# Spectral mix with a gated convolution: small transfers in place of the last row's products, a new order of work

## The chip, the core and the metric

The kernel runs on one core of one Trainium2 chip. The core has five engines with a queue of instructions each, which they work through in order: TensorE (PE in the profile; its weight loads are PEld), VectorE (DVE), ScalarE (ACT), GpSimd (POOL) and SyncE (SP, which here only issues DMA transfers). The metric is the device time of one execution in microseconds (us), as the median of several runs. One execution was also taken by the profiler; all rows shown come from that one.

## The reference

Two results are computed from the same input x (2048 positions, 512 channels, f32) and mixed by a gate:

```python
    x = A_x
    g = _sigmoid((x * gate_w).sum(-1, keepdims=True))
    a = _A_ref(x, A_w_r, A_w_i)     # rfft2, times a complex weight, irfft2
    b = _B_ref(x, ...)              # causal convolution over positions, plus x * D_skip
    return g * a + (1 - g) * b
```

The kernel of the convolution in b is made of 128 decaying exponentials for each channel. The program computes on the chip how many channels have exponents small enough (a bound on the exponent over all 2048 positions, below 2^-25) for the convolution to be a running sum of x times one number for each channel. With these inputs all channels do, and the general branch behind `tc.If(n_small < D)` isn't entered.

## The kernel before

Everything is f32. The two-dimensional transform a is done by matrix products. The work is cut into steps, each a small Python function that emits its instructions, and the order is written out by hand in the string `PLAN`: a letter for the step, then its numbers (which unit, then which buffers). `D6.1.0` is step D of unit 6, with PSUM bank 1 and block buffer 0. The order of the words is the order in each engine's queue; there is no other schedule. Waits between engines follow from the data. PSUM is used as four banks of two 512-column halves each, `ps0` to `ps3`. The block buffers (`pairs`, 8 KB a partition; `blk(i)` is half of one) and the `shorts` are shared by many steps, so a step also waits until the former user of its buffer is done.

The stages, in terms of the letters:

- `A` loads x in ten parts into GI; `C` (TensorE, line 233) makes the first transform along the positions, eight products of 128x128 for each of eight units, and `c` (ScalarE, line 238; one as `f` on VectorE) copies the bank to E1. All eight copies must be there before any `D`.
- `D` (line 248) transforms along the channels, eight products for each of eight units; `E` (253) copies the bank; `P` (269) finishes the transform along the positions into a bank; a ninth, half-sized unit (8) takes part from P on. `d` (275) copies two of a bank's eight parts; `Z` (290, 291, VectorE) forms sums and differences in place in the bank.
- `W` and `U` (311, 316, 317, VectorE) multiply by the complex weight, which `l` (299) has loaded into the part of GI that x no longer needs. Partition 127 of that weight, the row of channel frequencies 0 and 256, comes from a small extra table `hT` (steps `J`), which `L` (303, 305) puts in place with a small transfer from SP.
- `p` (321) adds the two halves of the weighted product by an accumulating DMA that GpSimd issues. `g` (328, 329, GpSimd) makes two sums and differences from it, 128x512 each.
- `I` (338, 339, 341, TensorE) transforms back along the channels. For partition 127 the sums of g aren't right: frequency 0 and frequency 256 share that row and need the bare parts and not their sums. So the matrix `dbw` has zeros in that row for the even outputs, and two further products (341) with 32 rows and 64 columns, from the uncombined data and the matrix `dbl`, bring the row in. `i` (346, ScalarE) copies the bank to GI.
- `B`, split for three units into `Y` and `b` (357, 358, 363), `T` (367, VectorE transposes), and `Q` (476) transform back along the positions; `q` (481, 482) adds the convolution's part and stores the result. Q multiplies by matrices that carry the gate: `a` loads their base, `K` (397, VectorE) multiplies by the gate, `k` (403, ScalarE) makes four copies with signs.
- The convolution: `X` loads x again with channels on partitions (XT), `m` (436, VectorE) makes the running sum, `s` (439, ScalarE) scales it, and two forms add it to XT times the skip term: `e` and `o` (442, VectorE, for two of the four channel groups), or `v` and `w` (445, ScalarE, scaling XT) and `M` (449, an accumulating DMA issued by GpSimd, for the other two groups). `H` (453, GpSimd) multiplies by 1 - g, eight times 128x1024. Every `q` needs all eight H.
- The gate: `G0` (375, TensorE) sums x times gate_w, `G1` (378, 379, ScalarE) takes g and 1 - g, `G2` stores both to DRAM (g by four transfers of scattered elements) and loads 1 - g broadcast to all partitions (`hg`); `G3` (389) loads g broadcast.
- `R`, `r` load constants and parameters; `N` decides which channels are small.

Of the kernel before, what the change touches and what calls it, by code (L numbers as in the profile page):

```python
# [15 lines left out]
P = 128  # L16
# [3 lines left out]
NPAIR = 8  # L20
# [20 lines left out]
def _consts():  # L41
# [100 lines left out]
def body(ctx: ExitStack, tc: tile.TileContext, x, xg, xt, w, wh, prms, vecs, gw, dskip,  # L142
# [19 lines left out]
    gd = wst.enter_context(tc.tile_pool(name="gdram", bufs=1, space=bass.MemoryType.DRAM)).tile([2, L], F32, name="gd")  # L162
# [33 lines left out]
    with tc.manual_schedule():  # L196
# [12 lines left out]
        def load_p(k, i):  # L209
# [9 lines left out]
            lambda: (nc.sync.dma_start(dbw, c_dbw[:, :, 0:2]), nc.sync.dma_start(dbl, c_dbw[96:P, :, 2])),  # L219
# [81 lines left out]
        def load_h(u, n):  # L301
            if u == 8:
                nc.sync.dma_start(wtile(8)[P - 1:P, :, :, 0].rearrange("p r a k -> p (r a) k"), hT[8:9, :, :64])
            else:
                nc.sync.dma_start(GI[P - 1:P, 8 * u:8 * u + 8 * n].rearrange("p (u n o) t -> p u n o t", n=4, o=2)[:, :, :, 0], hT[u:u + n])
# [16 lines left out]

        def g_a(u, i):
# [6 lines left out]

        def I_(u, i):
            m = nrow(u) // 64
            p = t_["pi", u] = bank(i).rearrange("p v (n t) -> p v n t", t=P)
            gt = t_["gt", u].rearrange("p h m c k -> p h m (c k)")
            px = t_["t", u][96:P, 0].rearrange("p x a (m k) -> p x a m k", k=64)
            for v in range(m):
                for h in range(2):
                    T.matmul(p[:, v, 2 * h + 1], gt[:, h, m + v], dbw[:, h, 1], start=True, stop=True)  # L338
                    T.matmul(p[:, v, 2 * h], gt[:, h, v], dbw[:, h, 0], start=True, stop=False)  # L339
                    for c in range(2):  # L340
                        T.matmul(p[64 * c:64 * c + 64, v, 2 * h], px[:, c ^ h, h, v], dbl[:, h], start=False, stop=True, tile_position=(96, 64 * c))  # L341
# [35 lines left out]
        def G1():  # L377
            S.activation(gsg[:, 0].rearrange("p (b a) -> p b a", a=16), t_["pg"].rearrange("p (a b) -> p b a", a=16), AF.Sigmoid)
            S.activation(gsg[:, 1], t_["pg"], AF.Sigmoid, scale=-1.0)

        def G2():
            nc.sync.dma_start(gd[1].rearrange("(j n) -> j n", j=4), gsg[0:P:32, 1])
            nc.sync.dma_start(hg, gd[1].rearrange("(o n) -> o n", o=1).broadcast_to([P, L]))
            for j in range(4):
                nc.sync.dma_start(gd[0].rearrange("(k b h a) -> k h b a", k=2, h=2, a=16)[j // 2, j % 2:j % 2 + 1], gsg[32 * j:32 * j + 1, 0].rearrange("p (b a) -> p b a", a=16))
# [49 lines left out]
        def scan(q):  # L435
            V.tensor_tensor_scan(run[:, q % 2, 1:1025], XT[:, 0, q], XT[:, 1, q], 0.0, op0=ALU.add, op1=ALU.add)  # L436
# [311 lines left out]
```

## Time and profile before

| | us |
|---|---|
| Median of 3 runs (lowest, highest) | 134.47 (134.28, 134.53) |
| The profiled execution | 134.16 |
| Its span in the profile | 132.4 |
| VectorE busy | 82.2 |
| ScalarE busy | 51.2 |
| GpSimd busy | 56.2 |
| First product starts | 4.86 |
| Last H ends, first q starts | 113.64, 113.67 |

The span runs from the first instruction to the last; the device time has 1.76 us more around it. A row of a timeline reads: start, duration, engine, line, operation, what it writes and reads, how many of them, and in brackets how long the engine was idle before and on what it waited. A `q` behind the engine's name (SPq) is the queue's own work, such as issuing a DMA; SP's time for issuing one is the duration shown, and the transfer lands later. A row of a window reads: start and end, its length, then each engine's busy time in it (PE, PEld, DVE, ACT, POOL in this order), the granted TensorE clock, the share in which the DMA engines were busy, and GB/s. A row of groups reads: line, engine, operation, tiles, shape, count, then busy time and the mean duration of one in ns, then idle time before them.

### The profile page before, as it was taken

The page shows a single profiled execution, that of the slowest core. Times are in us where ns is not written, and L with a number is a line of the kernel's source. Part 1 is how long each engine was busy: PE and PEld are TensorE (multiplying, and loading weights), DVE is VectorE, ACT ScalarE, POOL GpSimd, SP SyncE. Part 2 cuts the span into 40 slices and gives each one's busy share as a digit, 9 for nine tenths or more (in the row PEclk, how much of TensorE's full clock was granted, in tenths as well). Part 3 has the DMA queues.
Part 4 walks back from the last instruction along what each step waited for, and adds up shares of the span by engine and source line. Part 5 has one row for each costly group of instructions (what it writes and reads, how often), then busy time and mean ns, then how long its engine had stood idle before and what let it go on. Part 6 is the DMA issues. An engine that isn't in the chain of part 4 may idle for free.

```text
span 132.4 us, 2360 instructions
## 1 busy us (share of the span) xinstructions
PE 117.2 (89%) x944; PEld 95.5 (72%) x944; DVE 82.2 (62%) x101; ACT 51.2 (39%) x63; POOL 56.2 (42%) x49
## 2 busy tenths in 40 slices
PE   0599998999979999989999999999999999999700
PEld 0599997999879998858736766777655339999600
DVE  0031036078299999788770099999999573677610
ACT  3033635444267542313164113349679970000000
POOL 0000000001040840586798919499949999300000
PEclk9999999999999999999999999999999999999965
DMA  2999989996869789998667769990969600099660
GB/s 83 349 396 384 392 309 272 389 389 136 314 195 223 253 238 276 274 386 174 126 130 147 141 144 316 295 335 10 191 131 198 124 5 7 9 368 396 267 245 5
DMA packets 10643, 29.85 MB, mean 226 GB/s; under 512 B 1818, under 2 KB 2938, under 8 KB 10366
## 3 DMA queue, kind: packets, MB, share of 16 engines
q1 hardware_dynamic: 8606, 22.99, 48.4%
q0 software_dynamic: 1872, 6.55, 25.9%
q8 instruction: 9, 0.15, 0.4%
q10 hardware_dynamic: 144, 0.07, 0.4%
q14 instruction: 12, 0.10, 0.2%
HBM read 18.82 MB, written 4.21 MB: 174 GB/s over the span
## 4 chain that ended last, share of the span: by engine, by line
PE 69%; DMA 15%; DVE 7%; POOL 2%; issue 2%; ACT 1%
PE ps L233 13%; PE ps L476 12%; PE ps L357 11%; PE ps L338 9%; PE ps L341 8%; DMA blk<-blk 8%; PE ps L339 5%; PE ps L269 4%; DMA short<-in_prms_dram 3%; DMA GI<-in_x_dram 3%; PE ps L248 3%; PE ps L375 3%; DVE ps L290 2%; DVE ps L291 2%; DVE blk L316 1%
## 5 line engine op out<-in xcount | busy, mean ns | idle before, releaser
L233 PE MATMUL ps<-s,GI 128*128 128x128 f32 x128 | 17.4, 307 | 4.9 <-DMA GI<-in_x_dram 4.9
L453 POOL TENSOR_TENSOR XT<-XT,hg 128x1024 f32<-128x1024 f32 x8 | 20.9, 3038 | 0.0
L233 PEld LDWEIGHTS ps<-s,GI 128*128 128x128 f32 x128 | 17.2, 222 | 4.8 <-DMA s<-in_c_s_dram 4.8
L346 ACT COPY GI<-ps 128x1024 f32<-128x1024 f32 (+1 forms) x9 | 8.7, 964 | 24.2 <-PE ps L341 24.2
L328 POOL TENSOR_TENSOR blk<-blk 128x512 f32<-128x512 f32 (+1 forms) x9 | 13.0, 1443 | 11.6 <-DMA blk<-blk 11.2
L248 PE MATMUL ps<-dfw,E 128*128 128x128 f32 x128 | 15.6, 277 | 2.2 <-DVE blk L317 1.6
L248 PEld LDWEIGHTS ps<-dfw,E 128*128 128x128 f32 x128 | 14.8, 192 | 2.9 <-DVE blk L317 2.0
L338 PE MATMUL ps<-dbw,blk 128*128 128x128 f32 x68 | 16.3, 322 | 0.6 <-POOL blk L329 0.6
L269 PE MATMUL ps<-s2e,blk 128*128 128x128 f32 x136 | 16.8, 277 | 0.0
L269 PEld LDWEIGHTS ps<-s2e,blk 128*128 128x128 f32 x136 | 15.8, 192 | 1.2 <-issue 0.8
L357 PE MATMUL ps<-GI,s2p 128*64 128x512 f32 (+1 forms) x64 | 15.7, 583 | 0.0
L436 DVE TENSOR_TENSOR_SCAN run<-XT 128x1024 f32<-128x1024 f32 x4 | 11.2, 2803 | 6.7 <-DMA XT<-in_xt_dram 6.7
L476 PE MATMUL ps<-blk,E 128*128 128x128 f32 x128 | 15.3, 282 | 0.0
L476 PEld LDWEIGHTS ps<-blk,E 128*128 128x128 f32 x128 | 15.2, 196 | 0.1
L341 PE MATMUL ps<-last,blk 32*64 32x128 f32 x136 | 14.8, 293 | 0.0
L338 PEld LDWEIGHTS ps<-dbw,blk 128*128 128x128 f32 x68 | 10.1, 188 | 5.8 <-issue 5.0
L415 POOL TENSOR_TENSOR few<-few 128x4 f32<-128x4 f32 x1 | 0.2, 202 | 31.5 <-ACT few L412 31.5
L339 PE MATMUL ps<-dbw,blk 128*128 128x128 f32 x68 | 13.1, 275 | 0.0
L481 DVE TENSOR_TENSOR blk<-ps,XT 128x1024 f32<-128x1024 f32 x8 | 9.6, 1222 | 5.6 <-PE ps L476 2.8
L329 POOL TENSOR_TENSOR blk<-blk 128x512 f32<-128x512 f32 (+1 forms) x9 | 12.6, 1404 | 0.0
L238 ACT COPY E<-ps 128x1024 f32<-128x1024 f32 x7 | 7.1, 1012 | 13.7 <-PE ps L233 13.7
L311 DVE TENSOR_TENSOR blk<-ps,GI 128x1024 f32<-128x1024 f32 (+1 forms) x9 | 10.5, 1164 | 3.1 <-PE ps L341 1.8
(51 smaller groups left out, 142.7 us busy)
## 6 DMA issues: line engine op xcount, KB each, us to landing
XT<-in_xt_dram SPq DMA_DIRECT2D x4, 1024.0 KB, 6.6
GI<-in_w_dram SPq DMA_DIRECT2D x8, 512.0 KB, 3.9
blk<-blk POOLq DMA_DIRECT2D x8, 512.0 KB, 5.7
out_dram<-blk SPq DMA_DIRECT2D x8, 512.0 KB, 3.3
GI<-in_x_dram SPq DMA_DIRECT2D x6, 512.0 KB
XT<-run POOLq DMA_DIRECT2D x4, 512.0 KB, 5.9
GI<-in_x_dram SPq DMA_DIRECT2D x4, 256.0 KB, 5.4
hg<-gd SPq DMA_DIRECT2D x1, 1024.0 KB
```

Source lines behind the costliest of these rows:

```text
L233: T.matmul(p[:, u, :, j], X[:, 8 * k + 4 * u + j], s1, start=True, stop=True)
L248: T.matmul(p[:, n], E1[:, 8 * u + n], dfw[:, n % 4], start=True, stop=True)
L269: T.matmul(p[:, h, :, o, 64 * v:64 * v + 64], t_["e2", u % 8][:, 4 * v + 2 * h + o], st[:, ::-1] if h else st, start=True, stop=True)
L328: G.tensor_tensor(gt[:, :, :, 0], t[:, 0:4:3], t[:, 1:3], op=ALU.add)
L329: G.tensor_tensor(gt[:, ::-1, :, 1], t[:, 0:4:3], t[:, 1:3], op=ALU.subtract)
L338: T.matmul(p[:, v, 2 * h + 1], gt[:, h, m + v], dbw[:, h, 1], start=True, stop=True)
L339: T.matmul(p[:, v, 2 * h], gt[:, h, v], dbw[:, h, 0], start=True, stop=False)
L341: T.matmul(p[64 * c:64 * c + 64, v, 2 * h], px[:, c ^ h, h, v], dbl[:, h], start=False, stop=True, tile_position=(96, 64 * c))
L357: T.matmul(p[64 * s:64 * s + 64, u, :16 * n], s2p[:, 0, g], GI[:, 32 * s:32 * s + n, tt], start=True, stop=s == 1, tile_position=(0, 64 * s))
L436: V.tensor_tensor_scan(run[:, q % 2, 1:1025], XT[:, 0, q], XT[:, 1, q], 0.0, op0=ALU.add, op1=ALU.add)
L453: G.tensor_tensor(o, o, hg[:, 1024 * (k % 2):1024 * (k % 2) + 1024], op=ALU.mult)
L476: T.matmul(p[:, u, :, j], E4[:, b // 16, b % 16, :, u], t_["q", b // 8][:, 8 * u + b % 8].rearrange("p q a -> p (q a)"), start=True, stop= ...
```

## The change

Each word below says what the new program does in place of the old.

- **Zeros first.** `gsg` is cleared, and two products of 128x128 by 128x512 on it go to bank 3 before the plan starts.
- **Last row by small transfers.** `dbw` has its full rows again, `dbl` and line 341 are gone, so I is eight products for each full unit. A new step `h` runs between g and I: four transfers from SP, each of one partition, copy the uncombined parts over partition 127 of g's result.
- **L from ScalarE's queue** and not SP's.
- **Four sums on GpSimd.** For units 0, 1, 2 and 8 a new step `j` adds the halves by a GpSimd sum (128x1024, for unit 8 128x512) in place of the accumulating DMA `p`.
- **Skip terms by adding transfers.** The plan uses `v`, `w` and `M` for all four channel groups, and `e` and `o` for none. The running sums take block buffers (the tile `run` is gone, and there is a ninth pair of them). Since the shifted sum has no leading zero column any more, M of the even positions starts at the second column.
- **Gate turned on ScalarE.** Only 1 - g is computed, stored and broadcast. G3 makes g in the order that K wants with two copies `1 - hg` on ScalarE.
- **New order.** The plan is rewritten: all parts of x go out first, then XT 0, 3, 2, 1; C runs in the order 4, 3, 6, 1, 5, 7, 2, 0; D, P, W and I begin with 1, 2, 5, 3, 0; Q begins with 1, 3, 7.

```diff
-NPAIR = 8
+WARM = 2
+NPAIR = 9
...
-R0 A4 C3.0 A7 C6.1 r0.0 A3 c3 C2.0 r1.1 N0 A5 R3 J0 A6 C4.2 R8 A9 A8 c6 c2 C5.0 c4 f5 A1 C7.1 c7 A2 C1.0 R4 c1 A0 C0.1
...
-U3 G2 p3 g0.2 I4.3 a0.0 G5 Z8 W8.4 i4 I2.0 i2 a1.1 a2.2 I0.2 i0 U8 p8 g3.0 o0 e0 m2 e1 a3.3 g8.1 o1 I3.0 v2 s2 w2 i3
...
+R0 A5 C4.0 A4 A7 R4 A2 A6 C3.1 A9 A3 A0 A8 A1 c4 c3 X0 C6.0 R3 C1.1 X3 R1 R6 c1 X2 C5.2 c6 C7.1 m0.0 C2.0 c5 c7 X1 l2
+l1 c2 C0.1 c0 J0 r1.0 J1.0 m3.1 r0.1 D1.1.2 J2 E1 D2.0.3 E2 m2.4 R8 D5.1.5 m1.6 R10 r2.2 R2 P2.0 l0 l4 d2.3 l8 l3 l5
+l6 Z2 L1.2 N0 D3.2.7 E3 P1.3 G0.2 d1.3 N1 W2.8 U2 E5 N3 P3.0 G1 L3.2 D0.1.2 D4.2.3 d3.0 Z1 R5 W1.7 j2 E0 U1 R7 Z3 L0
+s1 g2.7 l7 P0.1 E4 j1 d0.0 W3.6 w1 v1 P5.3 U3 D6.0.8 G2 g1.9 Z0 W0.5 U0 h2 d5.0 Z5 L5.3 p3 D7.2.5 E6 M1 E7 P6.0 W5.8
+U5 h1 j0 w2 I1.1 d6.0 g0.8 P8.2 w3 v3 P4.3 i1 Z6 W6.7 U6 d4.0 Z4 W4.1 I2.1 P7.0 U4 p5 w0 s3 g3.9 N2 p6 M3 h3 d8.1 i2
+I3.1 p4 s2 d7.0 Z7 L8 g5.5 v0 s0 W7.6 g6.6 i3 v2 h5 h0 R9 a1.0 U7 Z8 W8.8 I0.0 p7 g4.7 h6 i0 U8 j8 a2.1 a0.2 I6.1 G3.7
+i6 I5.0 i5 h4 I4.2 i4 g8.8 g7.9 h8 K0 I8.0 G4.1 M0 i8 Y0.0 K1 Y1.2 h7 I7.3 H2 H3 G5 K2 i7 Y2.1 k0.8 b0 b1 a3.3 b2 K3
+T1 k3.7 T0 T2 B3.3 T3 M2 k2.6 k1.5 B7.2 B5.0 H6 T5 H7 H0 B4.1 B6.0 T7 H1 T4 Q1.2 Q3.1 T6 H4 Q7.0 H5 q1.0 Q6.2 q3.1
+q7.2 Q5.1 q6.3 Q2.0 q5.4 q2.5 Q4.1 Q0.0 q4.6 q0.7
...
-                nc.sync.dma_start(GI[P - 1:P, 8 * u:8 * u + 8 * n]...[:, :, :, 0], hT[u:u + n])
+                nc.scalar.dma_start(GI[P - 1:P, 8 * u:8 * u + 8 * n]...[:, :, :, 0], hT[u:u + n])
...
+        def j_a(u):
+            t = t_["t", u].rearrange("p r x a k -> p r (x a k)")
+            G.tensor_tensor(t[:, 0], t[:, 0], t[:, 1], op=ALU.add)
...
+        def h_a(u):
+            n = nrow(u)
+            t = t_["t", u][P - 1:P, 0, :, :, 0:n].rearrange("p x a (v k) -> p a x v k", k=64)
+            gt = t_["gt", u][P - 1:P, :, 0:n // 64].rearrange("p h v c k -> p h c v k")
+            for h in range(2):
+                for c in range(2):
+                    nc.sync.dma_start(gt[:, h, c], t[:, h, c ^ h])
...
-            for v in range(m):
-                for h in range(2):
-                    T.matmul(p[:, v, 2 * h + 1], gt[:, h, m + v], dbw[:, h, 1], start=True, stop=True)
-                    T.matmul(p[:, v, 2 * h], gt[:, h, v], dbw[:, h, 0], start=True, stop=False)
-                    for c in range(2):
-                        T.matmul(p[64 * c:64 * c + 64, v, 2 * h], px[:, c ^ h, h, v], dbl[:, h], start=False, stop=True, tile_position=(96, 64 * c))
+            for o in (1, 0):
+                for v in range(m):
+                    for h in range(2):
+                        T.matmul(p[:, v, 2 * h + o], gt[:, h, o * m + v], dbw[:, h, o], start=True, stop=True)
...
-            S.activation(gsg[:, 0].rearrange("p (b a) -> p b a", a=16), t_["pg"].rearrange("p (a b) -> p b a", a=16), AF.Sigmoid)
-            S.activation(gsg[:, 1], t_["pg"], AF.Sigmoid, scale=-1.0)
+            S.activation(gsg, t_["pg"], AF.Sigmoid, scale=-1.0)
...
-            nc.sync.dma_start(t_["gb"], gd[0].rearrange("(o n) -> o n", o=1).broadcast_to([P, L]))
+            o = t_["gb"].rearrange("p (k u b a) -> p u k b a", k=4, u=2, a=32)
+            v = hg.rearrange("p (u a k b) -> p u k b a", u=2, a=32, k=4)
+            for u in range(2):
+                S.activation(o[:, u], v[:, u], AF.Copy, scale=-1.0, bias=1.0)
...
         def both(q):
             for k in range(2):
-                G.dma_start(XT[:, k, q], run[:, q % 2, k:1024 + k], accum_op=ALU.add)
+                G.dma_start(XT[:, k, q, 1 - k:], t_["run", q][:, 0:1023 + k], accum_op=ALU.add)
...
-        V.memset(run[:, :, 0:1], 0.0)
+        V.memset(gsg, 0.0)
+        for k in range(WARM):
+            T.matmul(bank(3)[:, 0], gsg[:, 0:P], gsg, start=True, stop=True)
...
+            "W": W_, "U": U_, "p": p_a, "j": j_a, "g": g_a, "h": h_a, "I": I_, "i": i_a,
```

More of the change, by code (lines that the diff above doesn't have):

```diff
@@ L178, in body @@
     dbw = work.tile([P, 2, 2, P], F32, name="dbw")
-    last = work.tile([P, 4, P], F32, name="last")
-    hT, dbl = last[:9], last[96:P, 0:2]
+    hT = work.tile([9, 4, P], F32, name="hT")
     gws = work.tile([P, 4, 32], F32, name="gws")
-    gsg = work.tile([P, 2, 512], F32, name="gsg")
-    run = work.tile([P, 2, 1028], F32, name="run")
+    gsg = work.tile([P, 512], F32, name="gsg")
     pairs = [work.tile([P, 2, 1024], F32, name=f"blk{i}") for i in range(NPAIR)]
@@ L218, in body @@
             lambda: nc.sync.dma_start(eye, c_eye),
-            lambda: (nc.sync.dma_start(dbw, c_dbw[:, :, 0:2]), nc.sync.dma_start(dbl, c_dbw[96:P, :, 2])),
+            lambda: nc.sync.dma_start(dbw, c_dbw),
             lambda: nc.sync.dma_start(s2e[:, 2:8], c_s2e[:, 2:8]),
```

40 lines of the change are left out of this document (14 added, 26 removed).

## The prediction

> **What bounds the kernel now.** I read the busy shares first, then busy time by stage, then the chain of waits, then groups by shape and the timelines.
>
> ```profile
> span 132.4 us, 2360 instructions
> PE 117.2 (89%) x944; PEld 95.5 (72%) x944; DVE 82.2 (62%) x101; ACT 51.2 (39%) x63; POOL 56.2 (42%) x49
> ...
> GB/s 83 349 396 384 392 309 272 389 389 136 314 195 223 253 238 276 274 386 174 126 130 147 141 144 316 295 335 10 191 131 198 124 5 7 9 368 396 267 245 5
> ```
> ```profile
> 48.00:94.00 46.00, 45.43 (x379) 32.61 (x379) 35.93 (x46) 16.74 (x20) 31.94 (x26) 1.00 0.82 213
> ```
> TensorE is busy 117.2 of 132.4 us, and from 48 to 94 us 45.43 of 46.00. Nobody else is near that. So a cut in TensorE's work counts until another engine or queue becomes later. In the chain and in the groups by shape, the product with the dbw matrix stands out:
>
> ```profile
> 58.15 0.42 PE ps L338 x2
> 58.57 0.22 PE ps L339 x2
> 58.79 0.36 PE ps L341 x4
> ...
> 93.84 1.00 PE ps L357 x3
> ...
> 109.58 15.29 PE ps L476 x128
> ...
> 124.89 1.23 DVE blk L481
> ```
> ```profile
> 22.25 1.02 ACT E L238
> ...
> 23.31 3.84 PE ps L248 x32
> 27.15 1.80 PE ps L269 x16
> ...
> 28.97 0.59 ACT short L275
> ```
> Each f32 product is two instructions. A block of eight products is 16 instructions and takes 1.80 us in the last fence (0.112 us each), in C, D and P alike. One step of I (two full products, two 32x64 ones for the last row) takes 0.42 + 0.22 + 0.36 = 1.00 us, and there are 34 steps: 34 us. After I come B (93.84 to 109.58, 15.74 us), Q (15.29 us), and 132.4 - 124.89 = 7.51 us of last sum, store and end.
>
> **The change, part by part.**
>
> *Products of the last row leave TensorE.* Four instructions of 0.112 us remain per step: 34 x 0.45 = 15.2 us in place of 34, so up to 18.8 us of TensorE's time goes. By itself this would give 134.16 - 18.8 = 115.4 us, if everything else kept up. It doesn't.
>
> *Small transfers on SP.* In their place each of the nine units gets four transfers, each of one partition (two runs of 256 B), issued by SP behind the GpSimd step g and ahead of I. Nearest rows for the price:
>
> ```profile
> 28.49 0.87 SPq L305 DMA_DIRECT2D GI<-last  x1
> ...
> 50.73 1.09 SPq L223 DMA_DIRECT2D s2p<-in_c_s2p_dram  x1
> 51.87 0.46 SPq L223 DMA_DIRECT2D sgn<-in_c_sgn_dram  x1
> ...
> 61.05 0.62 SPq L303 DMA_DIRECT2D GI<-last  x1
> ...
> 77.33 0.35 SPq L383 DMA_DIRECT2D hg<-gd  x1
> 77.73 2.46 SPq L385 DMA_DIRECT2D gd<-gsg  x4
> 80.24 3.19 SPq L393 DMA_DIRECT2D short<-in_c_r_dram  x4
> ```
> ```profile
> s2e<-in_c_s2e_dram SPq DMA_DIRECT2D x1, 128.0 KB, 2.2
> ...
> XT<-run POOLq DMA_DIRECT2D x4, 512.0 KB, 5.9
> ```
> ```profile
> 31.45 1.22 DVE L311 TENSOR_TENSOR blk<-ps,GI 128x1024 f32<-128x1024 f32 x1
> ```
> Transfers that use few partitions took 0.62 us of SP each (L303, one row; the four of L385 in 2.46), at most 0.87; a plain broadcast 0.35. I take 0.62, from L303, which writes the same partition 127; bounds 0.35 and 0.87. Landing: the row transfer issued at 28.49 was used at 31.45, so 2.96 us at most; 128 KB landed in 2.2; an accumulating one of 512 KB, such as run beside these, took 5.9. I take 2.5, bounds 2.2 and 5.9. Nine units cost SP 36 x 0.62 = 22.3 us, in order, and in the plan h5, h0, both loads of R9, a1, h6, a2, a0, h4, h8 and h7 follow each other. h0's data is ready early, but it stands behind h5.
>
> [...]
>
> *Zeros first.*
>
> ```profile
> 4.86:8.62 3.76, 3.76 (x18) 3.76 (x19) 1.00 0.93 336
> 8.62:11.51 2.89, 2.89 (x18) 2.89 (x18) 1.00 1.04 402
> 11.51:13.29 1.78, 1.78 (x18) 1.78 (x18) 1.00 1.07 384
> ```
> ```profile
> L375 PE MATMUL ps<-XT,gws 128*32 128x512 f32 x32 | 3.6, 595 | 0.0
> ```
> The granted clock reads 1.00 throughout, yet C's first two blocks take 3.76 and 2.89 us where the third takes 1.78: 3.1 us lost in the first 5.8 us of activity. L375 runs 32 instructions of 512 columns, four side by side, in about 3.6 us: 0.45 us a pass; the zeros are four passes, at half pace 3.6 us, from an estimated 1.4 (after gsg is cleared) to 5.0, when x is there. If the slow time runs from the first product, it ends near 7.2, and C loses 1.2 us, not 3.1. Bounds: a gain of 0 (zeros don't count) and 3.1. I take 1.9, of which the chain below uses about 1.
>
> [...]
>
> *Order of loads, scans first.* All of x goes out first, then XT 0, 3, 2, 1 with dfw and six of the s2e blocks between: 8932 KB (9.15 MB) up to XT 1. The GB/s row has slices of 3.31 us: (83 + 349) x 3.31 is 1.43 MB by 6.6 us, and the rest at 390 GB/s takes 19.8 us: 26.4. The scan at 21.18 below waited for 6.26 MB in all, which by the same count (5.3 MB by 16.6 us, then 309 GB/s) were there at 19.6, so I add 1.5: 27.9.
>
> ```profile
> 21.18 2.29 DVE L436 TENSOR_TENSOR_SCAN run<-XT 128x1024 f32<-128x1024 f32 x1 [2.99 <-DMA XT<-in_xt_dram]
> ...
> 47.32 1.22 DVE L311 TENSOR_TENSOR blk<-ps,GI 128x1024 f32<-128x1024 f32 x1
> ...
> 51.51 1.22 DVE L311 TENSOR_TENSOR blk<-ps,GI 128x1024 f32<-128x1024 f32 x1
> ```
> ```profile
> L409 DVE TENSOR_REDUCE few<-short 128x4 f32<-128x512 f32 x2 | 1.4, 686 | 7.9 <-DMA short<-in_prms_dram 7.9
> L442 DVE SCALAR_TENSOR_TENSOR XT<-XT,few,run 128x1024 f32<-128x1024 f32 x4 | 8.5, 2166 | 0.0
> ```
> The last of four scans ends at 27.9 + 2.3 = 30.2. TensorE is ready sooner: C from 4.9, 8 x 1.79 + 1.2, copy 1.02, then D1, D2, D5, P2 (7.2) and copy 0.59 give 29.3. Without the zeros' help it would be 31.2: 1 us later.
>
> *VectorE.* It loses the four sums of L442 (8.5 us) and has its scans behind it, so from here it runs units Z, W, U at 51.51 - 47.32 = 4.19 us. Three reductions (0.69 each) stand between. U4, the seventh unit, ends at 30.2 + 7 x 4.19 + 2.1 = 61.6.
>
> *GpSimd.*
>
> ```profile
> 79.21 0.88 POOL L321 DMA_DIRECT2D blk<-blk  x1 [2.66 <-DVE blk L317]
> 79.83 1.57 POOL L328 TENSOR_TENSOR blk<-blk 128x512 f32<-128x512 f32 x1
> 81.05 1.56 POOL L329 TENSOR_TENSOR blk<-blk 128x512 f32<-128x512 f32 x1
> ...
> 99.04 14.60 POOL L453 TENSOR_TENSOR XT<-XT,hg 128x1024 f32<-128x1024 f32 x6
> ```
> g costs 2 x 1.22 = 2.44 us, an issue 0.62 (79.21 to 79.83), a 128x1024 sum 14.60 / 6 = 2.43, which I take for each j too (u = 8 half). Four j replace four issues: +6 us, against a landing (5 us and more) that nobody waits for now. The skip terms add four issues, 2.5 us, and four scalings on ScalarE. From U2 (35.8) GpSimd is almost never free: j2 g2 j1 g1 p3 M1 j0 g0 p5 g3 p6 M3, done near 59.5, then p4 waits for U4: 62.2, g5 64.7. With the rest (g6, p7, g4, j8, g8, g7, M0, eight H, M2) the last H ends near 99, counting that g8's buffer waits for I0.
>
> *ScalarE and rest.* Two gate copies and four scalings go to ScalarE (about 1.02 each, as its copies of that shape) and five row-transfer issues (0.62): some 9 us on 51. It stays near half busy. The row transfers wait there for their part of w; behind the first stand the copies E3 and d1, for which TensorE isn't waiting before 32 us, and w's parts 2 and 1 (1.05 MB more) are there by 30.6. I cost this at nothing; if w came 2 us later, W2 and all behind it would too. The gate's broadcast and its four scattered stores (SP 2.46 + 0.33) go.
>
> **The sum.** h5 is issued at 64.7. Ahead of the last transfer of h8 SP issues 19 small ones (11.8), R9 (1.6) and three c_r loads (3.19 / 4 each, 2.4): 80.5. Landed 83.0. I8 0.9, copy 0.59: 84.5. B 15.74, I7 (in its midst) 1.8: 102.0. Q 15.29, end 7.51: 124.8. TensorE from I6 on (landed 76.5) has I6, I5, I4, 5.4 us, and waits for h8. H (99) and its first sum are there before the fourth Q needs them (108). The profiled run took 134.16 us, 1.76 more than its span, so 126.6; the median of 134.47 is 0.3 above that run: **126.9 us**.
>
> **Rivals.**
> - *Cheap transfers* (0.35 a piece, 2.2 us): for it, SP is idle between loads; against, only 128-partition transfers were so cheap. Then h0 lands at 69.4, h6 at 72.2, and TensorE runs I0, I6, I5, I4, I8 on end: 121 to 123 us. Chance 0.22.
> - *The clock falls back in the pause.* TensorE waits from I3 (63) to h0 (71.6). If it restarts as slowly as at 4.86 us, and waits between I0, I6 and I4 keep it slow, I8 starts 2.9 us later: 129.8. For: the slow start; against: the longest pause of TensorE before, 1.29 us, has full pace (32 in 3.84) behind it, though none is as long as 8 us:
> ```profile
> 37.37 3.84 PE L248 MATMUL ps<-dfw,E 128*128 128x128 f32 x32 [1.29 <-DVE blk L317]
> ```
> [...] Chance 0.15.
> - *The engines alone*: transfers hidden, last H at 97, before's 18.8 us from H's end (113.64) to the span's end: 117.5. It needs h5 to h7 off SP's path, which the order speaks against. Chance 0.07.
> - *Slower.* One mechanism: SP's line h5 to h8. At 0.87 us a piece (19 x 0.25 = 4.8 more) and 5.9 landing (3.4 more) I8 starts 8.2 us later: 135.1. It decides from 7.6 us more. For: M3 and M0 move their bytes beside h3 and h8; against: the 2.96 us at 28.49, in a busy stretch. Chance 0.06.
> - *The zeros don't warm*: 1 us more; inside the range.
>
> **How the numbers follow.** The forecast with its bounds (from half way to 0.35 up to 0.87 a piece: 124.4 to 131.7) has 0.50. The range 120.5 to 131.7 takes in it, the cheap case and the pause, and leaves out the engines-only case and the slow one. Faster 0.93, same (within 0.2%, about what a measurement of this kernel can tell) 0.01, slower 0.06.
>
> **What would show it.** Right: SPq rows of the small transfers near 0.62 us, TensorE idle before I0 and I6 waiting for DMA, L338's block 1.8 us, g5 near 65, last H near 99, Q's start near 102. Wrong: no idle before I0 (cheap), blocks of 3.6 us after the pause (clock), U4 well off 61.6 (loads or VectorE), GpSimd later than Q.

## The result: 11% slower, and the profile after

The changed kernel takes 149.29 us (median of 4 executions, 149.19 to 149.71); the kernel before, run beside it, 134.50 (134.28 to 135.01). The ratio is 1.110, 95% interval 1.106 to 1.114. The forecast was 126.9 us, in a range from 120.5 to 131.7. Some executions of the kernels below took some per cent longer, most of them at a lower granted clock (e13: 155.05 us at a mean of 0.88, 150.79 at 0.92): times and ratios leave these out, but the rows shown of e11 and e13 are of such executions.

The page of the changed kernel (line numbers are now those of the new program: C 228, I 345, h 336, g 327 and 328, B and Y 361 and 362, T 371, K 400, count 436, H 459, Q 482):

```profile
span 147.8 us, 2164 instructions
PE 112.1 (76%) x812; PEld 93.2 (63%) x812; DVE 88.4 (60%) x96; ACT 58.8 (40%) x69; POOL 60.9 (41%) x53
...
PEclk9999999999999999699755899559856999999955
...
L345 PE MATMUL ps<-dbw,blk 128*128 128x128 f32 x136 | 20.6, 310 | 17.3 <-DMA blk<-blk 12.9
```
The row of the granted clock in the kernel before:

```profile
PEclk9999999999999999999999999999999999999965
```
TensorE was busy for 117.2 of 132.4 us before. It is busy for 112.1 now, only 5.1 less although by the prediction's sum 18.8 us of products are gone, and the span is 15.4 longer. The first two lines thus give two questions: why the remaining products take longer, and why TensorE stands idle. The rows of the clock answer the first in part: it was full up to TensorE's last products before, and is now down to half in several stretches. The last row of the changed kernel begins the second: I, line 345, waited 12.9 us for a transfer between block buffers, and in this place of the program that is h.

TensorE's timeline from 73 us on, with the waits in brackets:

```profile
73.02 2.05 PE L345 MATMUL ps<-dbw,blk 128*128 128x128 f32 x8 [3.87 <-DVE blk L312]
79.26 3.84 PE L345 MATMUL ps<-dbw,blk 128*128 128x128 f32 x18 [4.19 <-DMA blk<-blk]
...
83.86 3.81 PE L345 MATMUL ps<-dbw,blk 128*128 128x128 f32 x32 [0.76 <-DMA blk<-blk]
89.83 1.35 PE L345 MATMUL ps<-dbw,blk 128*128 128x128 f32 x10 [2.16 <-DMA blk<-blk]
93.08 1.19 PE L345 MATMUL ps<-dbw,blk 128*128 128x128 f32 x4 [1.90 <-DMA blk<-blk]
...
94.95 1.97 PE L361 MATMUL ps<-GI,s2p 128*64 128x512 f32 x4 [0.41 <-ACT GI L350]
...
101.20 2.05 PE L345 MATMUL ps<-dbw,blk 128*128 128x128 f32 x16
108.37 1.97 PE L361 MATMUL ps<-GI,s2p 128*64 128x512 f32 x4 [5.12 <-DVE count L436]
```
I's odd outputs need no h, so each wait for h stands in front of or inside a unit's even half: of I0 (79.26), I6 (83.86), I4 (89.83) and I8 (93.08). A fifth, 3.94 us of I1, ends at 57.84. After I8 come Y0 and Y1, I7 (101.20), and then 5.12 us of waiting for `count`, a single number that VectorE copies. It isn't late by itself. It stands behind another instruction, as VectorE's and GpSimd's timelines show:

```profile
87.12 21.14 DVE L400 TENSOR_TENSOR short<-short,blk 128x512 f32<-128x512 f32 x2 [9.19 <-DMA short<-in_c_r_dram]
108.18 0.14 DVE L436 CAST count<-ps 1x1 int32<-1x1 f32 x1
108.25 1.27 DVE L400 TENSOR_TENSOR short<-short,blk 128x512 f32<-128x512 f32 x2
```
```profile
L400 DVE TENSOR_TENSOR short<-short,blk x4: 669/676/20534, 87.1 to 108.8; 128x512 f32<-128x512 f32 x4
```
```profile
86.23 5.27 POOL L459 TENSOR_TENSOR XT<-XT,hg 128x1024 f32<-128x1024 f32 x2
...
91.97 15.12 POOL L459 TENSOR_TENSOR XT<-XT,hg 128x1024 f32<-128x1024 f32 x6
```
The two K at 87.12 take 21.14 us together, and the next two, of the same shape, 1.27. By the view of line 400 (shortest, median and longest in ns) it is a single K that took 20.53 us: the first, from 87.12 to 107.65. Line 459 is H on GpSimd; it runs from 86.23 to 107.09 with one gap of 0.5 us, and the long K ends 0.56 us after it. It is the same in three of the runs below: the long K of e1, e3 and e9 (22.02, 20.33 and 19.20 us) ends 0.55 or 0.56 us after the last H each time. K gets in neither between two H nor in the gap.

The small transfers themselves, in the view by line: shortest, median and longest issue on SP in ns, and who waited for them (us, times):

```profile
L336 SPq DMA_DIRECT2D blk<-blk x36: 552/558/1384, 45.0 to 94.3; - x36
...
  PE ps L345: 12.9, 5
```

### The profile page after: what moved, and what is told of

Same layout as the page of the kernel before. It is cut to its first block, busy times and chain, and to the rows that moved or that the text cites. A ratio compares the mean times of both kernels' runs of the same rounds, so it can differ in the third digit from the quotient of the medians.

```text
span 147.8 us, 2164 instructions
## 1 busy us (share of the span) xinstructions
PE 112.1 (76%) x812; PEld 93.2 (63%) x812; DVE 88.4 (60%) x96; ACT 58.8 (40%) x69; POOL 60.9 (41%) x53
## 4 chain that ended last, share of the span: by engine, by line
PE 37%; DMA 28%; DVE 12%; issue 10%; SPq 4%; POOL 2%; ACT 0%; POOLq 0%; ACTq 0%; DVEq 0%
DMA GI<-in_w_dram 11%; PE ps L482 10%; PE ps L228 9%; PE ps L361 8%; DVE short L400 6%; DMA GI<-hT 5%; DMA blk<-blk 5%; DMA gd<-gsg 4%; SPq L336 3%; PE ps L264 3%; DMA short<-in_c_r_dram 3%; PE ps L495 3%; PE ps L345 2%; DVE blk L306 2%; DVE ps L286 1%
## 5 line engine op out<-in xcount | busy, mean ns | idle before, releaser
L345 PE MATMUL ps<-dbw,blk 128*128 128x128 f32 x136 | 20.6, 310 | 17.3 <-DMA blk<-blk 12.9
L345 PEld LDWEIGHTS ps<-dbw,blk 128*128 128x128 f32 x136 | 18.7, 218 | 18.6 <-DMA blk<-blk 11.5
L400 DVE TENSOR_TENSOR short<-short,blk 128x512 f32<-128x512 f32 x4 | 22.4, 5638 | 9.2 <-DMA short<-in_c_r_dram 9.2
L361 PE MATMUL ps<-GI,s2p 128*64 128x512 f32 (+1 forms) x64 | 19.9, 700 | 5.5 <-DVE count L436 5.1
L459 POOL TENSOR_TENSOR XT<-XT,hg 128x1024 f32<-128x1024 f32 x8 | 20.4, 3458 | 0.0
L440 DVE TENSOR_TENSOR_SCAN blk<-XT 128x1024 f32<-128x1024 f32 x4 | 9.2, 2292 | 18.8 <-DMA XT<-in_xt_dram 18.8
L228 PEld LDWEIGHTS ps<-s,GI 128*128 128x128 f32 x128 | 15.4, 203 | 1.4 <-DMA s<-in_c_s_dram 1.4
L243 PEld LDWEIGHTS ps<-dfw,E 128*128 128x128 f32 x128 | 14.6, 192 | 2.5 <-DVE blk L312 1.5
L228 PE MATMUL ps<-s,GI 128*128 128x128 f32 x128 | 15.6, 287 | 0.0
L482 PE MATMUL ps<-blk,E 128*128 128x128 f32 x128 | 15.3, 282 | 0.0
L327 POOL TENSOR_TENSOR blk<-blk 128x512 f32<-128x512 f32 (+1 forms) x9 | 11.5, 1277 | 3.5 <-DMA blk<-blk 2.3
L371 DVE STREAM_TRANSPOSE E<-ps 128x1024 f32<-128x1024 f32 x8 | 9.4, 1225 | 5.5 <-PE ps L367 3.9
L362 PEld LDWEIGHTS ps<-GI,s2p 128*64 128x64 f32 x32 | 5.1, 160 | 10.4 <-issue 10.1
```

The lines of the kernel that those rows point to most:

```text
L228: T.matmul(p[:, u, :, j], X[:, 8 * k + 4 * u + j], s1, start=True, stop=True)
L243: T.matmul(p[:, n], E1[:, 8 * u + n], dfw[:, n % 4], start=True, stop=True)
L327: G.tensor_tensor(gt[:, :, :, 0], t[:, 0:4:3], t[:, 1:3], op=ALU.add)
L345: T.matmul(p[:, v, 2 * h + o], gt[:, h, o * m + v], dbw[:, h, o], start=True, stop=True)
L361: T.matmul(p[64 * s:64 * s + 64, u, :16 * n], s2p[:, 0, g], GI[:, 32 * s:32 * s + n, tt], start=True, stop=s == 1, tile_position=(0, 64 * s))
L371: V.transpose(E4[:, g, :, 32 * j:32 * j + 32].rearrange("p b t k -> p t b k"), t_["pb", k].rearrange("p u (s t) -> p u t s", t=16))
```

## The experiments

Three theories were on the table at first: that h's transfers in SP's line cost the time (A in the expectations), that K beside H does (B), and that the new order does (C). From e5 on D says that A and B add up. Other letters are rivals that each expectation describes. All ratios are to the kernel before on the same chip, with 95% intervals.

**e1: the row left out.**

```diff
         def h_a(u):
+            return
```


> The changed kernel without its 36 small transfers (step h); the row of frequencies 0 and 256 is left out, nothing takes their place. Theory A (SP's line of small transfers is what costs: it makes I late, keeps buffers from W8 and from the gate, holds back the loads of c_r, and so pushes K beside the H multiplies): I1 no longer waits for a transfer (2.2 us earlier U4), K is done before the H start, GpSimd becomes the bound: 122 us, 119 to 126. Theory B (K meets H whatever the transfers do, VectorE starves beside GpSimd): K's 20 us row stays, 139 to 145. Theory C (the new order and the row transfers from ScalarE's queue cost most): above 135, with U4 still ending after 66 us.

144.35 us, ratio 1.070 (1.062 to 1.079). The row of VectorE shows what took the place of the waits for h:

```profile
85.52 23.27 DVE L398 TENSOR_TENSOR short<-short,blk 128x512 f32<-128x512 f32 x2
```
With h gone, the first two K and the count come before H, and the other two K are caught by it: 23.27 us for two, 22.02 of them for the second. Y now waits 13.4 us for a transpose queued behind them. The time lies where B had it, and A alone isn't the answer.

**e2: K on GpSimd.**

```diff
-            V.tensor_tensor(t_["r", j], t_["r", j], t_["gb"][:, 512 * j:512 * j + 512], op=ALU.mult)
+            G.tensor_tensor(t_["r", j], t_["r", j], t_["gb"][:, 512 * j:512 * j + 512], op=ALU.mult)
```


> The changed kernel with the four K multiplies on GpSimd ahead of its H in the same order, and nothing else. If VectorE's K is starved by GpSimd's H: the pause of TensorE at 103 to 108 us goes and with it the half pace behind it, GpSimd ends 5 to 7 us later without being the bound: 142 us, 140 to 144 (theory A: only this last link goes, the rest of the lateness stays). Theory B as the whole cause: below 136. If K waits for something else (a load, a buffer), nothing is gained: 149 to 152.

137.49 us, 1.020 (1.013 to 1.026), between the branches expected and 11.8 us less than the changed kernel, though GpSimd has four more instructions and its last H ends at 115.24. Not all of this is K's price. I8 starts 4.3 us earlier (88.78 in place of 93.08), since SP's last twelve issues (h4, h8, h7) go through faster; first the changed kernel, then e2:

```profile
83.97 10.98 SPq L336 DMA_DIRECT2D blk<-blk  x12
```
```profile
83.21 8.46 SPq L336 DMA_DIRECT2D blk<-blk  x12
```
GpSimd's K stand ahead of its adding transfers M0, which go out at 88.12 in place of 85.08, behind h8 and no longer beside it. In the changed kernel h8's four issues take 1.08 to 1.38 us each, and the second transfer lands 5.2 us after its issue began; in e2 they take 0.52 to 0.58, and it lands after 1.7. The price of K stands behind that: from I7's start to Q's start it is 14.6 us (94.67 to 109.25) in place of 21.9 (101.20 to 123.05). Q then waits for the late H and takes 1.7 us more.

**e6: H left out, K where it was.**

```diff
-                G.tensor_tensor(o, o, hg[...], op=ALU.mult)
+                pass
```


> The changed kernel without the eight H multiplies; the convolution's part is left without its factor 1 - g. If H is what starves K: the four K rows take 0.7 us each, at 87 to 89 us and after the last load, the pause at 103 to 108 is gone, TensorE alone sets the end: 138 us, 135 to 141. If K waits for something else, a row of about 20 us stays and so does the time, 147 to 150.

```profile
88.23 1.29 DVE L400 TENSOR_TENSOR short<-short,blk 128x512 f32<-128x512 f32 x2 [8.93 <-ACT blk L393]
...
99.55 0.67 DVE L400 TENSOR_TENSOR short<-short,blk 128x512 f32<-128x512 f32 x1
100.89 0.69 DVE L400 TENSOR_TENSOR short<-short,blk 128x512 f32<-128x512 f32 x1 [0.67 <-DMA short<-in_c_r_dram]
```
All four K take 0.67 to 0.69 us: it is H that stretches them. The time, however, is 146.4 us, 1.097 (1.088 to 1.107), only 3 us less than the changed kernel where 11 were expected. I8's last product starts at 98.33 here (in the changed kernel its whole even half ran from 93.08), behind h8: SP's last twelve issues took 12.65 us. GpSimd without H issues all four adding transfers of M0 and M2 from 86.22 on, beside h8, whose issues take 0.89 to 1.42 us and whose second transfer lands 6.7 us after its issue began. H can't be what slows them, since it is gone. What the slow h8 have in common, here and in the changed kernel, is adding transfers in flight; in e2, where M0 goes out behind h8 at 88.12, its issues take 0.52 to 0.58 us. No run moves these transfers alone. From I7's start to Q's start it is 14.4 us (106.34 to 120.71) here too, so K's price is gone, and most of it is lost again ahead of I8.

**e5: K early, H and the row as in the change.** G3 takes another buffer, the loads a, K and the count stand ahead of H.

```diff
-... p6 M3 h3 ...  i3 v2 h5 h0 R9 a1.0 U7 ... j8 a2.1 a0.2 I6.1 G3.7 i6 ... K0 I8.0 ... K1 ... G5 K2 ... a3.3 b2 K3
+... R9 a0.4 a2.2 a3.3 p6 M3 h3 ... s2 G3.5 ... W7.6 a1.0 ... j8 K0 K2 K3 K1 I6.1 ... G4.1 G5 M0 ...
```


> The changed kernel, with the small transfers, but the gate copies, the loads of c_r, K and the copy of count moved ahead of the H in the plan (g kept in a buffer that is free from 55 us, one more short buffer). Theory D (two losses that add up: the SP line makes I8 10 us later than forecast, and K beside H costs 11 us more, 5 of pause and the rest of half pace and waiting): only the second goes, K rows are below 3 us each, Y to Q run without a pause: 138 us, 135 to 141. Theory B alone (K is all that went wrong): 127 to 131. If VectorE is starved by any GpSimd work, the g sums too, K is still late and little is gained: 144 to 149.

```profile
79.32 4.53 DVE L400 TENSOR_TENSOR short<-short,blk 128x512 f32<-128x512 f32 x4
...
102.28 4.64 DVE L371 STREAM_TRANSPOSE E<-ps 128x1024 f32<-128x1024 f32 x4 [8.93 <-PE ps L367]
```
138.56 us, 1.044 (1.028 to 1.061), as D had it. The four K are done before H starts at 88.67, and from I7's start to Q's start it is 14.4 us (97.54 to 111.91). The second row is worth a look: beside the same H (88.67 to 109.65) VectorE's transposes T, which read PSUM, take 4.64 / 4 = 1.16 us; in the changed kernel, where T comes after H, the first four take 4.65. Of the two only K, with two inputs from SBUF, was stretched, in the changed kernel to 20.53 us in place of 0.67. Whether it is the inputs or the operation that makes them differ, no run shows.

**e11: half of the transfers.** As e5, with two of the four transfers of each unit left out.

```diff
-            for h in range(2):
+            for h in range(1):
                 for c in range(2):
                     nc.sync.dma_start(gt[:, h, c], t[:, h, c ^ h])
```


> e5 (K early, row by transfers) with two of the four transfers of each unit left out, so 18 in place of 36; half of the last row's even part keeps g's value. If what costs is their number in SP's in-order queue (the issues between g and I, and the loads behind them), half of it goes: 139.2 falls to 134 (132 to 136). If it is the landing of the last one behind each g, or the waits in SP's line, the time stays within 1.5 of 139.2.

128.87 us, 0.966 (0.959 to 0.972), where 132 to 136 was expected. The number of transfers counts. It counts early as well: in e5 SP needs 10.05 us for the first eight issues, 4.3 of them waiting for a transfer of L to land, and gives the loads behind them out after 55.10; here

```profile
45.26 2.70 SPq L336 DMA_DIRECT2D blk<-blk  x4
48.01 0.39 SPq L218 DMA_DIRECT2D s2p<-in_c_s2p_dram  x1
```
the first four take 2.70 us and the load follows at 48.01. I0 begins at 73.78 (76.75 in e5) and Q's products at 108.03 (111.91).

**e7: the kernel before, with the row by transfers alone**, each h right ahead of its I in the old order.

> The kernel before with one part of the change alone: the last row by four small transfers from SP, each unit's right ahead of its I in the old order, full rows in dbw, no products of line 341. If the row part pays by itself (18.8 us of TensorE against the line of transfers): U8 near 70 us, GpSimd's H end near 106, 127 us, 122 to 131. If the transfers eat it all: 134 or above. If they are hidden: 116 to 120.

142.80 us, 1.082 (1.062 to 1.101), where 127 was expected and 134 or more was the other branch. From this run's waits (us, times, longest):

```profile
PE ps L342 <- DMA blk<-blk: 20.4, 7, 8.3
...
POOL blk L324 <- PE ps L342: 13.0, 2, 6.7
```
TensorE waits 20.4 us for the row, more than the 18.8 that the products took, and GpSimd's next g waits for the I whose buffer it needs. So the transfers make even the old order slower.

**e3: no zeros.** `WARM = 0`.

> The changed kernel without the two products on zeros. If the zeros are what lets C run at full pace from its first block (13.66 us for the eight blocks here, 17.4 before), C loses 3.1 us and so does the first Z behind it: 152.5 us, 151 to 153.5. If the loads of XT hide it: 149.3.

150.9 us, 1.123 (1.115 to 1.131), between the two branches: the zeros are worth about 1.6 us.

**e4: the row by ScalarE.** Two copies of partitions 96 to 127 before g in place of h; g's sums for the even outputs leave partition 127 alone, so they are four GpSimd operations.

```diff
+            S.copy(gt[96:P, :, :v, 0], t[96:P, 0:4:3, :v])
+            S.copy(gt[96:P, ::-1, :v, 1], t[96:P, 1:3, :v])
...
+            for m, q in ((slice(v, 2 * v), P), (slice(0, v), P - 1)):
+                G.tensor_tensor(gt[:q, :, m, 0], t[:q, 0:4:3, m], t[:q, 1:3, m], op=ALU.add)
+                G.tensor_tensor(gt[:q, ::-1, m, 1], t[:q, 0:4:3, m], t[:q, 1:3, m], op=ALU.subtract)
```


> The changed kernel with the last row put in place in another way: no transfers; ScalarE first copies partitions 96 to 127 of the uncombined parts (two copies of 32 x 256 for each unit), and GpSimd's sums for the even outputs then write partitions 0 to 126 only (four operations of half the size in place of two). Theory A: as without the transfers, plus at most 2 us on GpSimd for the smaller operations: 124 us, 120 to 129. Theory B: 139 to 145, K still beside H. Theory C: above 135.

134.97 us, 1.003 (0.996 to 1.011), above A's range and below B's. K falls ahead of H by itself (85.1 to 92.1). GpSimd now ends last, at 114.8: g4 waited 5.61 us for p4.

**e8: both mended.** e4's row, e5's K, M3 behind p7, and some loads and row copies earlier.

> The row by ScalarE's copies as in e4, K and its loads and the count ahead of the H as in e5, the adding transfers M3 behind p4 and p7 in GpSimd's queue, w's part 3 loaded ahead of parts 0 and 4, and the row copies of units 2, 3 and 8 earlier on ScalarE. Theory D with GpSimd as the next bound: p4 lands in about 5 us rather than 13, GpSimd does not wait 5.6 us before g4, last H near 104: 124 us, 121 to 129. If the accumulating transfers are slow for another reason than M3 in front of them: 131 to 135.

127.99 us, 0.964 (0.952 to 0.976), below both kernels and inside the expected range.

```profile
span 125.9 us, 2112 instructions
PE 104.0 (83%) x812; PEld 88.2 (70%) x812; DVE 73.2 (58%) x96; ACT 65.5 (52%) x87; POOL 65.5 (52%) x71
...
PEclk9999999999999999999999658999999999999975
```
**e12: e8 with M3 in front of p4 and p7 again.**

> e8 (128.0) with one edit taken back: the skip terms' adding transfers M3 (two of half a MB) stand ahead of p4 and p7 in the adding queue again, as in the changed kernel. If they hold up p4 (which landed 11 to 13 us after its issue behind them in e4, about 5 elsewhere), g4 and I4 come later and the time is 131 (130 to 133); if p4 has slack now that the row needs no transfers, 128 within 0.7.

127.79 us, 0.957 (0.950 to 0.963). Not slower than e8: the place of the adding transfers has no price here.

**e9 and e10: the row by products again, in the new order**, without h. e10 has K early too.

> The changed kernel with one part undone: the last row is made by products on TensorE again (line 341 of the kernel before, 136 of them, 18.8 us by the prediction's row), the 36 row transfers are gone; new order, zeros, four sums, skip terms by adding transfers and the gate on ScalarE stay. Theory D (two losses: SP's line of row transfers, and K beside H): the first loss goes and the products come back, the second stays, since K still stands beside H in the order: K rows far over 0.68 us, Y or Q waits for them, time 141 to 150. Rival E (the row's transfers are the whole loss): K is short, 130 to 136. Rival F (the new order itself is the loss, whatever the row does): above 150.

> As the run before, and with G3, the loads a, K and the count ahead of H (the edit of e5). Theory D: neither loss is left, the products are paid: TensorE is the bound again as in the kernel before, which it beats by the zeros' 1.6 us at most: 133 (130 to 136). By it the row costs the changed kernel nothing against products in this order only if e5 (139.2) is not slower than this run; I expect e5 to be slower by 6. Rival F (the order or the adding transfers of the skip terms lose time by themselves): 138 or more.

155.74 us, 1.165 (1.154 to 1.177), and 156.41, 1.176 (1.165 to 1.186). Both lie above D's ranges, by 6 and by 20 us, and in the branch of rival F, that the new order loses by itself; but e8, in nearly the same order, is faster than the kernel before. K early brought nothing. The windows of e10 (start and end, length, PE busy, PEld, DVE, ACT, POOL, clock, DMA share, GB/s) show why:

```profile
66.00:70.00 4.00, 2.21 (x19) 1.60 (x18) 1.17 (x2) 4.00 (x3) 3.79 (x7) 1.00 0.69 131
70.00:74.00 4.00, 3.62 (x21) 2.27 (x20) 2.00 (x5) 3.28 (x5) 4.00 (x6) 0.59 0.93 172
...
78.00:108.00 30.00, 30.00 (x138) 20.72 (x136) 3.28 (x7) 4.05 (x4) 25.81 (x19) 0.50 0.60 118
...
112.00:116.00 4.00, 4.00 (x30) 2.17 (x27) 0.00 (x0) 0.00 (x0) 0.07 (x1) 1.00 0.02 6
```
TensorE is busy for every one of the 30 us from 78 to 108, at half the clock. It fell at about 71, behind a pause of 1.79 us that ended at 68.34, and came back at about 111, when Y had replaced I. At full pace those 30 us would be 15, an estimate from the clock of 0.50.

**e13: e10 with the pauses filled** by products that nobody reads: 6 ahead of I3, 9 ahead of I0.

```diff
+            "y": lambda n, i: [T.matmul(bank(i)[:, 0, 0:P], dbw[:, 0, 0], dbw[:, 0, 1], start=True, stop=True) for _ in range(n)],
```


> e10 (products for the row, K early, 156.9) with its two pauses of TensorE from 66 to 76 us filled: 6 products of 128x128 that nobody reads stand ahead of I3 (into the bank that I3 writes next) and 9 ahead of I0 (into a bank free until the end of the stage). If the fall of the granted clock to 0.50 at 70.7 us, which lasts to 111, is the loss and follows from the pauses: the clock stays at 1.00 and the time falls by half of the 40 us at half pace, to 137 (134 to 141). If the clock falls for another reason (the products of 32 rows and 64 columns themselves), 153 or more.

```profile
74.00:78.00 4.00, 3.13 (x27) 2.56 (x27) 3.81 (x8) 1.68 (x2) 4.00 (x5) 1.00 1.09 197
78.00:82.00 4.00, 4.00 (x22) 2.72 (x22) 2.74 (x7) 0.27 (x1) 1.18 (x2) 0.56 1.05 234
82.00:108.00 26.00, 25.59 (x123) 17.27 (x123) 0.65 (x2) 4.36 (x5) 24.53 (x18) 0.50 0.56 106
```
150.08 us, 1.126 (1.099 to 1.154), between the two branches: filling the pauses gained about 4%. In the execution that these rows show the clock held through both pauses, and fell at 78.4 instead, in the middle of I0, with a remaining pause of 0.87 us before it. Its mean clock was 0.88; two others, of which there are no rows, had 0.92 and 0.93, so the clock was down for less of their time. So it isn't shown that the pauses alone explain it. These products alone don't: in the kernel before, I runs from 75.66 to 93.77 without a break at a clock of 1.00. What is shown is that once the clock was down, it stayed down through 33 us of this mix of full and 32x64 products without a pause (e10, 76.29 to 108.94), while in the changed kernel I's full products had it back within 3.2 us (79.26 to about 82.4). What brings it down at 78.4 stays open.

**e14: e8 with 24 such products** ahead of I0. **e15: e8 with G3 later**, so that Z7 isn't kept waiting. **e16: both**, with 12 products.

```diff
-... s2 G3.5 d7.0 ... i3 v2 U7 Z8 W8.8 I0.0 ...
+... s2 d7.0 ... i3 G3.5 v2 U7 Z8 W8.8 I0.0 ...
```


> e8 (128.0) with 24 products that nobody reads ahead of I0, in the pause of TensorE from 64.7 to 72.2 us. If the clock of 0.50 from 70 to 77 us follows from this pause: it stays at 1.00, the row's products from 72.2 on run at full pace, and TensorE, which is busy from there to its end, ends 2.4 us earlier: 125.8 (125 to 127). If GpSimd sets the end (the last H at 107.4) or the clock does not answer: 128 within 0.7.

> e8 with one step moved: G3 (3.8 us on ScalarE at 63.5 us), in front of the copy that Z7 waits for, stands behind i3. Z7 to U7 come 3.7 us earlier, so that bank 0 is free and I0 starts at 68.5 in place of 72.2; TensorE's pause is then 4 us. K starts later, about 77, and still ends ahead of H. If TensorE sets the end: 124.5 (123 to 127). If GpSimd's sums and H do (they start no earlier, since g5 waits for p5's landing): 127.5 to 128.5.

> e15 with 12 products that nobody reads in the pause of about 4 us ahead of I0. By the clock's theory up to 1.5 below e15 where e15's clock falls to 0.50, the same where it does not fall: 123.5 (122 to 127).

128.84 us, 0.964 (0.940 to 0.988); 126.41, 0.948 (0.935 to 0.961); 126.06, 0.949 (0.931 to 0.966). The same windows of e8 and then of e14:

```profile
68.00:72.00 4.00, 0.00 (x0) 0.00 (x0) 3.81 (x7) 3.93 (x7) 3.60 (x6) 0.74 0.33 92
72.00:76.00 4.00, 3.75 (x17) 3.78 (x18) 3.81 (x9) 2.30 (x4) 4.00 (x7) 0.50 0.55 103
```
```profile
68.00:72.00 4.00, 1.86 (x17) 1.66 (x15) 3.81 (x8) 3.92 (x7) 3.69 (x6) 1.00 0.33 92
72.00:76.00 4.00, 3.83 (x34) 3.86 (x35) 3.81 (x9) 3.23 (x5) 4.00 (x7) 1.00 0.60 113
...
84.00:88.00 4.00, 4.00 (x15) 1.66 (x16) 0.00 (x0) 0.00 (x0) 4.00 (x5) 0.57 0.39 73
```
The clock of 0.50 from 72 to 76 us in e8 follows from the pause ahead of it, 7.58 us: filled up to a rest of 2.31 us, it stays at 1.00. But I ends hardly earlier, since it then waits 2.15 us for g (on GpSimd), and the clock falls one stage later. The expected 2.4 us don't come. e15's interval overlaps with e8's; its median and e16's are the lowest, and the two can't be told apart.

## Why the prediction was wrong

The forecast was a sum along one chain; the changed kernel's rows give its terms:

| | Forecast | Measured |
|---|---|---|
| g5 done | 64.7 | 72.0 |
| from there to I8's products | 18.3 | 21.1 |
| I8's start to Q's start | 19.0 | 30.0 |
| Q | 15.3 | 15.3 |
| Q's end to the span's end | 7.5 | 9.4 |
| Span | 124.8 | 147.8 |

- **What held.** Up to 36 us the forecast was right: zeros (1.9 us forecast, about 1.6 by e3), the last scan (30.2, measured 29.6), U2 (35.8, measured 35.2). The issue of a small transfer was 0.62 us against a median of 0.56.
- **VectorE's row of units, U4 at 61.6, was wrong by 6.4 us.** (VectorE runs its units in the order 2, 1, 3, 0, 5, 6, 4; of D, P, W and I only D begins with 1, 2, 5, 3, 0.) It was costed at 4.19 us for each unit with no wait. Its waits are:

```profile
44.50 1.23 DVE L306 TENSOR_TENSOR blk<-ps,GI 128x1024 f32<-128x1024 f32 x1 [2.34 <-DMA gd<-gsg]
...
54.43 1.23 DVE L306 TENSOR_TENSOR blk<-ps,GI 128x1024 f32<-128x1024 f32 x1 [1.59 <-DMA GI<-hT]
...
63.76 0.43 DVE L285 TENSOR_TENSOR ps<-ps,short 128x256 f32<-128x256 f32 x1 [2.23 <-ACT short L270]
```
  The second waits for the row of w that L brings (issued by ScalarE at 48.87). The first names another transfer, but e8 shows the same W3 waiting 2.53 us for that same row. Both come from "I cost this at nothing": the prediction looked at the first L only. The third, 2.23 us, is Z4, whose product P4 stands behind I1 in TensorE's queue, and I1 waited 3.94 us for h1. The early h (h2, h1, h3) stand nowhere in the sum. The eight issues of h2 and h1 take 0.55 to 0.72 us each, yet they stretch over 9.69 us, because SP had to wait for other transfers to land:

```profile
SPq L336 <- DMA hg<-gd: 3.0, 1, 3.0
...
SPq L336 <- DMA GI<-hT: 1.6, 1, 1.6
```
  In the trace the last two issues of h1 wait for the semaphores that the gate's broadcast (issued at 44.58) and L's transfer (48.87) count up when they land, and then count up the same two; no data ties them. With 0.52 in front of W6 the waits of VectorE make 6.7 us, and p4 and g5 came later with U4.
- **SP's line** was foreseen. It began 7.3 us late, with g5, and was 2.8 us too long, 21.1 against 18.3, by its landing. I8's even half starts behind h8's second transfer, which was issued 15.7 us after g5 was done (forecast for the last: 15.8) and landed 5.2 us after its issue began, where 2.5 was taken. Over all 36 the landing took 1.6 to 6.0 us. The slower rival named the place, M0 beside h8, and its bound of 5.9 was near; it took 0.87 a piece, and h8's issues took 1.08 to 1.38. What it lacked is the late start and K.
- **The step that failed most is the one that isn't there: K beside H.** The prediction put K nowhere in its sum: from I8 to Q it added copy, B and I7, 19.0 us with no wait, and measured are 30.0. It checked H only against Q. VectorE's and GpSimd's timelines of the kernel before have all four K in one row, and one H beside it:

```profile
93.58 4.59 DVE L397 TENSOR_TENSOR short<-short,blk 128x512 f32<-128x512 f32 x4
```
```profile
92.85 2.97 POOL L453 TENSOR_TENSOR XT<-XT,hg 128x1024 f32<-128x1024 f32 x1
```
  They were done at 98.17, before the six H in a row that begin at 99.04 (quoted in the prediction), and beside a single H. The sign was there: the first of the four took 2.78 us, to 0.54 us after that H, and the others 0.68. In the change I8 is late and the loads a are late in SP's line, so K meets eight H in two blocks. In VectorE's queue the count stands behind two K; it starts at 108.18, after the long one, and Y2 waits for it. The price is 7.3 to 7.5 us: from I7's start to Q's start it is 21.9 us here, and 14.6, 14.4 and 14.4 in e2, e5 and e6, where K isn't beside H. 5.1 of it is the wait, the rest the half clock behind it.
- **The clock** was a rival with a chance of 0.15, for the pause between I3 and h0. The fall is there, in more places than that. The windows of the changed kernel:

```profile
72.00:76.00 4.00, 2.05 (x8) 1.78 (x8) 1.97 (x6) 0.54 (x1) 3.21 (x3) 0.52 0.96 184
...
96.00:100.00 4.00, 4.00 (x15) 1.34 (x13) 4.00 (x1) 0.00 (x0) 4.00 (x3) 0.57 0.78 165
108.00:112.00 4.00, 3.63 (x13) 1.95 (x15) 1.52 (x4) 4.00 (x7) 0.00 (x0) 0.50 0.01 4
```
  TensorE is at half pace after its pauses, in Y0 and Y1 and again in B. From 94.95 to about 99.5 and from 108.37 to about 113.1 this costs half of the time, 4.6 us in all, an estimate from the granted clock in windows of 1 us. e5, at 1.00 in both places, agrees in the main: from Y0's start to I7's it takes 4.0 us (93.50 to 97.54) in place of 6.3 (94.95 to 101.20). The first half of this stands behind waits for h, the second behind the wait for K, in whose price it is counted above. How long a pause must be, the runs don't settle: the clock fell to 0.50 behind one of 1.79 us (e10), while 2.31 us in e14 and 1.29 us in the kernel before left it at 1.00.
- **M3 ahead of p4** wasn't costed either. e12 shows no price for it in the mended order; in the changed kernel itself it wasn't tried alone.
- **The 18.8 us that TensorE was to gain** are there where the row costs the chain little: e8 has TensorE busy 104.0 us, 13.2 less than before, with 3.7 us for the zeros and some 4 us at half pace in it. The time of about 127 us is what e8 reaches, by another way to make the row and with K early; it doesn't bear out the forecast's sum.

The loss thus comes in two parts: the ratio of 1.110 falls to 1.044 when K stands early (e5), and to 0.966 when half of the row's transfers go as well (e11). Q's end to the span's end, 1.9 us longer, I didn't follow up.

## What to carry to other kernels

When an engine loses work, cost what stood beside it as well: here the new order put K beside H, and an instruction of 0.67 us became one of 20.5. Look at single instructions and not at a row's mean: 2.78 us beside one H was hidden in a row of four. Many small transfers in one queue can cost more than their issue, here 0.56 us in the middle: two of h1's waited 3.0 and 1.6 us for others to land, h8's second landed 5.2 us after its issue began with adding transfers in flight (1.7 in e2), and the load behind the first ones went out at 55.10 with eight of them (e5) and at 48.01 with four (e11). And a pause of TensorE wasn't paid once: behind that of 5.12 us its products ran at a clock of 0.50 until about 113.1.

## What the runs showed of the hardware

- In the changed kernel a VectorE product of 128x512 with two SBUF inputs took 20.5 us, against 0.67, beside eight GpSimd products of 128x1024 with one gap of 0.5 us, and ended 0.56 us after the last of them; transposes out of PSUM beside the same products took 1.16 us (e5).
- The granted clock fell to 0.50 behind pauses of TensorE of 1.79 us (e10) and 7.58 us (e8), and not behind one of 2.31 us (e14). It stayed there through 33 us of unbroken work (e10) when that work was the mix of 128x128 and 32x64 products.
- In the changed kernel a transfer of 512 bytes in one partition took SP 0.56 us to issue in the middle, and up to 1.23; four of 256 bytes took 1.08 to 1.38 with adding transfers in flight, and 0.52 to 0.58 without them (e2). The 36 landed 1.6 to 6.0 us after their issue began.
